# Query weights transposed by DMA, bias rows in two column tiles, FFN weight loads as steps of a new order list

## Chip, cores and metric

The kernel runs on one core of a Trainium2 chip. The metric is the device time of one execution in microseconds (us), the median of several runs. A core has a tensor engine (PE, with its weight loads listed apart as PEld), VectorE (DVE), ScalarE (ACT), GpSimd (POOL) and SyncE (SP); each works through its own queue of instructions in order. In this kernel nearly all DMAs are issued from SP's queue.

## The reference

One transformer block with modulation from a conditioning row. S = 2048 tokens, D = 576, H = 32 heads of 18, FFN width 4608, all in bfloat16:

```python
mod = (silu(c) @ w_mod).reshape(1, 6, 1, D)
sa, ca, ga, sb, cb, gb = (mod[:, i] for i in range(6))
h = layernorm(x) * (1 + ca) + sa
x = x + ga * A(h)
h = layernorm(x) * (1 + cb) + sb
out = x + gb * (relu(h @ w1) @ w2)

def A(h):
    q, k, v = split_heads(h @ wqkv)                    # 32 heads of 18
    pq, pk = q @ w_phi[head], k @ w_phi[head]          # 18 x 18 for each head
    phi_q = concat(softmax(pq), softmax(-pq))          # 36 features
    phi_k = concat(softmax(pk), softmax(-pk))
    kv, z = sum_s(phi_k * v), sum_s(phi_k)             # linear attention, not causal
    return merge_heads((phi_q @ kv) / (phi_q @ z + 1e-6)) @ wo
```

## The kernel before

**Tiles and stages.** The 2048 tokens are 16 tiles t of 128; two tiles make a unit of 256 tokens (n = 0 to 7), four make a block of four tiles. A first phase folds the weights, projects keys and values of all tiles, takes the key softmaxes, sums KV over all tokens and does unit 0 of attention and FFN. Then `block(n)`, n = 1 to 7, does the FFN of unit n with the attention of unit n + 1 between. The seven blocks take the last 272 us of the span, from 151.7 us on. The change lies in the first phase.

**The order of the work.** The first phase is a string of steps, `order`; each word names a function in the table `steps`, with its arguments behind dots, and emits its instructions at once. Each engine runs its instructions in this order, SP's DMAs among them; a semaphore holds an instruction until its operands are there, and all that is queued behind it on that engine waits too. So a word's place in the list fixes where its work stands in every queue.

**Folded weights.** The head maps `w_phi` and the modulation (1 + ca, sa) are folded into the projections, so that one product of the normalized, transposed tile (`hT`) gives the features. For the keys: load the raw rows (`LK.i`), transpose them on PE in six groups of 108 columns, that is six heads (`WT.ci`, `fold_T`, L320; `GRP` has the group starts), copy them to SBUF (`WTE`, L85 on ACT or L87 on DVE, tile `wT`), multiply each group with a block-diagonal matrix of its heads' maps (`F1.ci`, `fold`, L330; the matrix `wbd` is made by `WBD`, `feature_maps`), copy out (`FA1`, `FB1`, into `wplain`), scale by 1 + ca (`SC1`, into `wfold[1]`). For the queries: load the raw rows (`LQ`, 648 KB in two DMAs into a part of the tile `room`), then `QT.ci`, `QTE`, `F0.ci`, `FA0`, `FB0`, `SC0` in the same way, into `wfold[0]`. The value weights are only scaled (`SCv`). There are five row chunks ci, of 128 rows, the last of 64.

**Bias rows.** The shift sa, multiplied with the unscaled folded weights, makes one further row of each folded weight (row 64 of chunk 4, met by a constant 1 in `hT`). `B1`, `Bv`, `B0` (`fold_bias`, L350) compute it for keys, values and queries: two halves of 288 columns by five chunks, ten products with a left operand `sal` of 65 columns, of which only the last holds sa; `BE1`, `BEv`, `BE0` copy that row out on ACT, both halves at once.

**Tiles to transposed tiles.** `LS` statistics, `RS` the root, `LX` the normalized tile `xn`, then `LT.t` a transposing DMA of SP (L227) or, for units 0 and 1, `PT` on PE. `LP` and `LP4` load x for two and four tiles, `LA` and `LM` the modulation weights, `LV` the value weights, `WOL` the output weights. `K.t`, `V.t`, `Q.t` (`project`, `proj`, L406) are ten products each; `KE`, `VE`, `QE` copy them out on ACT.

**From KV to the FFN of unit 0.** `KVa`, `KVb`, `KVc` sum keys by values (L585), `KVE` copies them to SBUF with the heads' mask. `qT.n` transposes the query features of unit n with two DMAs (L613, tile `ET`); `NU.j`, `NV.j` (L626) multiply them with KV for units 0 and 1, and `NUE`, `NVE` divide on DVE (L634 to L641). `WS.ci` scales the output weights (`wo_sb`, L372) by a row that lives in the tile group `wm`; the next tile group at that address holds the FFN weights `w1a` and `w1c`, so their load waits for the last `WS`. `WO`, `WP` are output products. `G.g` (L759, L767) is the first FFN product of group g with its pairs of 64-row products that read `w1c`; `FW.q` (L767) the further ones, q up to 4 on `w1a`, later ones on `w1b`. `Y.j.h.p` (L810) is the second FFN product of tile j, half h, twelve of the 36 chunks k in part p; it reads `w2` (tile `w_sb`), of which each load brings nine chunks.

**FFN weight loads before.** `W1` (`weights_1`, L717 to L719) opens the tiles and issues at once two DMAs for `w1c` and two for `w1a` (8 and 12 of its 20 column blocks); `P2` (`open_p2`, L739, L742) issues the one for `w1b` and four for `w2`. All stand in SP's queue with `qT.1` behind them.

Of the kernel before, what the change touches and what calls it, by code (L numbers as in the profile page):

```python
# [43 lines left out]
def kernel(  # L44
# [271 lines left out]
    def fold_T(which, ci):  # L316

        ps = pool_tiles["T", which, ci] = mm_tile("ps_wT")[:, 0].bitcast(BF16)
        for g, h0 in enumerate(GRP):
            T_.transpose(ps[0:G6, g * P:(g + 1) * P], wraw[which][:, ci, h0 * DH:h0 * DH + G6], ident[:])  # L320
# [24 lines left out]
    def fold_bias(which, src):  # L345

        ps = pool_tiles["B", which] = mm_tile("ps_bias")
        for half in range(2):
            for ci in range(KC):
                T_.matmul(ps[0:65, half, 0:288], lhsT=sal[:, ci, :], rhs=src[:, ci, half * 288:(half + 1) * 288],  # L350
                          start=(ci == 0), stop=(ci == KC - 1))
# [358 lines left out]
    def weights_1():  # L710
# [4 lines left out]
        w1r = B_w1[512:576, :].rearrange("k (j e n) -> k j e n", e=2, n=P)  # L715
        for e in range(2):
            nc.sync.dma_start(w1["c"][e * 64:e * 64 + 64], w1r[:, :, e, :])  # L717
        for lo, hi in ((0, 8), (8, JH)):
            nc.sync.dma_start(w1["a"][:, :, lo * P:hi * P],  # L719
                              B_w1[0:512, lo * P:hi * P].rearrange("(k p) n -> p k n", p=P))  # L720

# [11 lines left out]
    def open_p2():  # L733
# [5 lines left out]
        nc.sync.dma_start(w1["b"][:], B_w1[0:512, JH * P:].rearrange("(k p) n -> p k n", p=P))  # L739
        p2t["w2"] = p2.tile([P, NJ, D], BF16, name="w2_sb")  # L740
        for q in range(4):
            nc.sync.dma_start(p2t["w2"][:, q * 9:(q + 1) * 9, :],  # L742
                              B_w2[q * 9 * P:(q + 1) * 9 * P, :].rearrange("(j p) d -> p j d", p=P))
# [258 lines left out]
```

## Time and profile before

| what | value |
|---|---|
| time, median of 3 runs (lowest to highest) | 425.34 us (425.01 to 426.44) |
| the profiled execution's own time | 425.97 us |
| its span, first to last instruction | 423.6 us |
| granted TensorE clock | 1.00 |

Busy time in stretches of the span, from the trace, in us:

| stretch | PE | DVE | ACT | DMA share |
|---|---|---|---|---|
| 0 to 24 | 19.79 | 17.32 | 15.60 | 0.96 |
| 24 to 48 | 21.58 | 19.90 | 15.13 | 0.73 |
| 48 to 88 | 40.00 | 38.63 | 37.83 | 0.09 |
| 88 to 130 | 40.17 | 26.24 | 24.52 | 1.04 |
| 130 to 160 | 29.89 | 19.72 | 5.33 | 0.30 |
| 160 to 424 | 260.77 | 111.57 | 78.11 | 0.20 |

The first two rows are loading and folding, the third projections and softmaxes, the fourth KV and unit 0 with the FFN weights coming in. The rest are the seven blocks. A row's busy time against its length says how long an engine stood still there; which wait that was is read from the waits of that stretch. A DMA share near 1 says that the sixteen DMA engines always had packets under way. The page lists 4030 products on PE.

### The profile page before, as it was taken

To read this page: it belongs to the slowest core of one execution; us is meant where nothing else is said; L and a number is where in the kernel's file an instruction comes from. 1 tells how busy PE (TensorE), PEld (TensorE's weight loads), DVE (VectorE), ACT (ScalarE), POOL (GpSimd) and SP (SyncE) were. 2 spreads that over 40 slices of the span, in tenths; PEclk is the share of its full clock that TensorE was granted. 3 is DMA by queue.
4 is the path that set the end of the run, shared out by engine and by line. 5 is a ranking of instruction groups with operands and counts; after the bars stand their busy time and mean duration, and the time that the engine had idled before them with its cause. 6 is when DMAs were issued, how large, how long until landed. Compare 5 with 4: busy or idle time off the path is not lost.

```text
span 423.6 us, 9341 instructions
## 1 busy us (share of the span) xinstructions
PE 412.2 (97%) x4030; PEld 338.5 (80%) x4030; DVE 233.4 (55%) x613; ACT 176.5 (42%) x282; POOL 14.6 (3%) x41
## 2 busy tenths in 40 slices
PE   6988999999998999999999999999999999999997
PEld 5876777787786788878878887888888788878886
DVE  6879899999616574528462834555284623230011
ACT  4767899965742126204520540262045204402400
POOL 8300000000000000000000000000000000000000
...
DMA  8997130059995401232041207201420412010000
GB/s 245 355 225 126 33 62 2 2 72 323 380 316 100 102 16 33 33 82 46 2 83 46 33 2 115 31 17 31 84 47 2 84 44 33 2 45 15 2 2 28
DMA packets 68105, 34.90 MB, mean 82 GB/s; under 512 B 53985, under 2 KB 65314, under 8 KB 68066
## 3 DMA queue, kind: packets, MB, share of 16 engines
...
HBM read 19.64 MB, written 2.36 MB: 52 GB/s over the span
## 4 chain that ended last, share of the span: by engine, by line
PE 84%; DMA 7%; SPq 5%; DVE 2%; ACT 1%; issue 0%; DVEq 0%
PE ps_y L810 33%; PE ps_h L767 26%; SPq L742 4%; PE ps_v L406 4%; PE ps_h L759 4%; PE ps_k L406 4%; PE ps_q L406 3%; DMA ET<-room 3%; PE ps_wo L683 3%; PE ps_sum L472 3%; DMA hT<-xn 2%; PE ps_kv L585 1%; DMA oT<-o_tm 1%; PE ps_num L626 1%; PE ps_wo L406 1%; PE ps_bias L350 1%
## 5 line engine op out<-in xcount | busy, mean ns | idle before, releaser
L772 ACT ACTIVATE H<-ps_h 128x1024 bf16<-128x1024 f32 x72 | 73.6, 1022 | 179.0 <-PE ps_h L759 123.8
L810 PE MATMUL ps_y<-w_sb,H 128*128 128x288 bf16 (+2 forms) x1188 | 142.8, 282 | 0.0
L810 PEld LDWEIGHTS <-H 128*128 128x128 bf16 x1188 | 113.7, 98 | 27.3
L767 PE MATMUL ps_h<-hT,w1a 128*128 128x256 bf16 x640 | 74.9, 273 | 0.4 <-DVE hT L377 0.4
L767 PEld LDWEIGHTS <-w1a 128*128 128x128 bf16 x640 | 61.4, 98 | 9.7 <-issue 2.4
L818 DVE TENSOR_TENSOR outt<-ps_y,row_gb 128x288 bf16<-128x288 f32 (+2 forms) x33 | 14.8, 448 | 87.3 <-PE ps_y L810 87.3
L767 PE MATMUL ps_h<-hT,w1b 128*128 128x256 bf16 x512 | 59.2, 273 | 0.0
L406 PEld LDWEIGHTS <-hT 128*128 128x128 bf16 x480 | 46.2, 97 | 13.8 <-DMA hT<-xn 2.1
L767 PEld LDWEIGHTS <-w1b 128*128 128x128 bf16 x512 | 49.7, 98 | 6.8 <-issue 0.8
L688 DVE TENSOR_TENSOR x_sb<-x_sb,ps_wo 128x288 bf16<-128x288 bf16 x28 | 12.7, 454 | 34.3 <-PE ps_wo L683 24.8
L203 DVE BATCH_NORM_STATS2 bst<-x_sb 128x6 f32<-128x288 bf16 x64 | 25.8, 445 | 0.9 <-DMA x_sb<-in_A_x_dram 0.9
L212 DVE TENSOR_SCALAR xn<-x_sb,mv,rstd 128x576 bf16<-128x576 bf16 x32 | 12.3, 430 | 21.0 <-ACT rstd L208 21.0
L406 PE MATMUL ps_v<-wv_sb,hT 128*128 128x288 bf16 x160 | 21.7, 286 | 1.1 <-DMA hT<-xn 1.1
L406 PE MATMUL ps_k<-wfold,hT 128*128 128x270 bf16 (+1 forms) x160 | 21.1, 285 | 0.6 <-DMA hT<-xn 0.6
L406 PE MATMUL ps_q<-wfold,hT 128*128 128x270 bf16 (+1 forms) x160 | 21.3, 285 | 0.0
L759 PE MATMUL ps_h<-hT,w1c 64*128 64x256 bf16 x288 | 19.9, 271 | 0.0
L465 ACT ACTIVATE room<-room 128x1188 bf16<-128x1188 bf16 x16 | 19.0, 1187 | 1.6 <-DVE room L438 1.1
L465 ACT ACTIVATE phik<-phik 128x2376 bf16<-128x2376 bf16 x8 | 17.4, 2181 | 0.3 <-DVE phik L438 0.3
L482 DVE TENSOR_REDUCE ln_s<-room 128x66 f32<-128x1188 bf16 x12 | 16.4, 1363 | 0.0
L759 PEld LDWEIGHTS <-w1c 64*128 64x128 bf16 x288 | 12.1, 94 | 5.2 <-issue 3.8
L425 DVE TENSOR_TENSOR tree<-tree 128x264 bf16<-128x264 bf16 (+2 forms) x48 | 14.6, 304 | 1.7
L634 DVE TENSOR_SCALAR rq<-ps_num 128x24 f32<-128x24 f32 (+1 forms) x18 | 3.0, 177 | 20.1 <-PE ps_num L626 20.1
...
## 6 DMA issues: line engine op xcount, KB each, us to landing
w_sb<-in_B_w_dram SPq DMA_DIRECT2D x4, 1296.0 KB, 18.4
...
w1b<-in_B_w_dram SPq DMA_DIRECT2D x1, 2048.0 KB, 15.3
...
```

The costliest lines, as they stand in the source:

```text
L203: V.bn_stats(out=st[:, half, :], in_=x_sb[:, t0 + j, half * 288:(half + 1) * 288])
L406: T_.matmul(ps[:, 0:cn], lhsT=lhs[:, ci, :], rhs=w[:, ci, cs:cs + cn], start=(ci == 0), stop=(ci == KC - 1))
L425: V.tensor_tensor(out=a[:, :, 0:w], in0=a[:, :, 0:w], in1=a[:, :, w:2 * w], op=op)
L465: A_.activation(out=E[:, j:j + k], in_=E[:, j:j + k], func=ACT.Exp)
L472: T_.matmul(ps, lhsT=ident[:], rhs=e[:, :, :, f * G2:(f + 1) * G2], start=(f == 0), stop=(f == DH // 2 - 1))
L482: V.tensor_reduce(out=t["l", 0][:, j * 22:(j + 1) * 22].rearrange("p (g s) h -> p g s h", s=2), op=ALU.add, axis=mybir.AxisListType.X, in_ ...
L742: nc.sync.dma_start(p2t["w2"][:, q * 9:(q + 1) * 9, :], B_w2[q * 9 * P:(q + 1) * 9 * P, :].rearrange("(j p) d -> p j d", p=P))
L759: T_.matmul(f1[q][:, e, hh * w:hh * w + w], lhsT=w1["c"][r, 2 * q + hh, :], rhs=hT[r, 4, :], start=(first and hh == 0), stop=(not first an ...
L767: T_.matmul(f1[q][:, e, hh * w:hh * w + w], lhsT=w1_at(4 * q + 2 * hh + e, ci), rhs=hT[:, ci, :], start=(first and hh == 0 and ci == 0), s ...
L772: A_.activation(out=p2t["H1"][:, 4 * q:4 * q + 4, :].rearrange("p (h e) n -> p e h n", e=2), in_=f1[q][:].rearrange("p e (h n) -> p e h n" ...
L810: T_.matmul(ps[:, 0, 0:cn], lhsT=p2t["H1"][:, k, j * P:(j + 1) * P], rhs=p2t["w2"][:, k, c], start=(k == 0), stop=(k == NJ - 1))
L818: V.tensor_tensor(out=o[:, c], in0=ps[:, 0, 0:cn], in1=rows["gb"][:, c], op=ALU.mult)
```

## The change

1. **Query weights.** `LQ` is now six steps. Each is one transposing DMA that reads 128 columns of `A_wqkv` in DRAM, from column 108 g on, and writes group g of `wqT`. The load of the raw query rows, `QT` and `QTE` are gone; `fold_T` serves the keys alone. So that the groups start at equal distances, the last one starts at head 30 instead of 26: the key rows are padded with zeros to 668 columns, and the last group of `wph` holds only two heads' maps, with zeros behind.
2. **Bias rows.** The left operand `sal` is one column. The two halves of each bias row go to PSUM partition 64 and to partition 0, and their products alternate. Each half is copied out by its own step, on DVE (`.0` at the end) or ACT (`.1`).
3. **FFN weights.** `W1` and `P2` open the tiles only. `LW.0` and `LW.1` load the halves of `w1c`, `LW.2` and `LW.3` those of `w1a`, `LW.4` loads `w1b`, `W2.q` a quarter of `w2`.
4. **The order list** is another one throughout. Among much else, x and the key rows are loaded in another order, all `WS` come around and behind `KVc`, `LW.3` is the first of the FFN weights, `W2.1` stands behind `qT.1`, and one step `Z.8` adds one product on zeros. `block` is as before.

```diff
-GRP = [0, 6, 12, 18, 24, 26]
+GRP = [0, 6, 12, 18, 24, 30]
 KK = [P, P, P, P, 64]
 NGR = len(GRP)
 G6 = 6 * DH
+DX = 5 * G6 + P
...
-    wv_raw, wq_raw, wqT = part(0, KC, D), part(KC * D, KC, D), part(2 * KC * D, NGR, D)
-    wq_plain = part((2 * KC + NGR) * D, KC, D)
-    o = (3 * KC + NGR) * D
-    wbd, sal = part(o, NGR, G6), part(o + NGR * G6, KC, 65)
+    wv_raw, wqT, wq_plain = part(0, KC, D), part(6752, NGR, D), part(10208, KC, D)
+    o = KC * D
+    wbd, sal = part(o, NGR, G6), room[:, o + NGR * G6:o + NGR * G6 + KC]
...
-    wraw = {1: p0.tile([P, KC, D], BF16, name="wk_raw"), 0: wq_raw}
+    wk_raw = p0.tile([P, KC, DX], BF16, name="wk_raw")
...
+    V.memset(wph[:, 5, :], 0.0)
...
-    A_.dma_start(wph[0:G6, 5, :], wphr[D - G6:])
+    A_.dma_start(wph[0:36, 5, :], wphr[5 * G6:])
...
-            nc.sync.dma_start(wraw[1][:, 2 * i:2 * i + 2, :], rows)
+            nc.sync.dma_start(wk_raw[:, 2 * i:2 * i + 2, 0:D], rows)
         else:
-            nc.sync.dma_start(wraw[1][0:64, 4, :], A_wqkv[512:576, D:2 * D])
+            nc.sync.dma_start(wk_raw[0:64, 4, 0:D], A_wqkv[512:576, D:2 * D])
+
+    def load_turned(which, g):
+        c0 = which * D + g * G6
+        nc.sync.dma_start_transpose(out=wT[which][:, g, :], in_=A_wqkv[:, c0:c0 + P])
...
-    zero_rows(wraw[1])
+    G.memset(wk_raw[:, :, D:], 0.0)
+    G.memset(wk_raw[64:128, 4, 0:D], 0.0)
...
-        for g, c, h, nh in ((slice(0, 5), 0, 0, 3), (slice(0, 5), GF, 3, 3), (slice(5, 6), 0, 4, 2)):
+        for g, c, h, nh in ((slice(0, 5), 0, 0, 3), (slice(0, 5), GF, 3, 3), (slice(5, 6), 0, 0, 2)):
...
-        V.tensor_copy(out=sal[:, 0:4, 64], in_=mod_ps[1][:, 0:4])
-        V.tensor_copy(out=sal[0:64, 4, 64:65], in_=mod_ps[1][0:64, 4:5])
+        V.tensor_copy(out=sal[:, 0:4], in_=mod_ps[1][:, 0:4])
+        V.tensor_copy(out=sal[0:64, 4:5], in_=mod_ps[1][0:64, 4:5])
...
-    def fold_T(which, ci):
-
-        ps = pool_tiles["T", which, ci] = mm_tile("ps_wT")[:, 0].bitcast(BF16)
-        for g, h0 in enumerate(GRP):
-            T_.transpose(ps[0:G6, g * P:(g + 1) * P], wraw[which][:, ci, h0 * DH:h0 * DH + G6], ident[:])
-
-    def fold_T_out(which, ci, eng):
-        copy(eng, wT[which][0:G6, :, ci * P:ci * P + KK[ci]],
-             pool_tiles["T", which, ci][0:G6, 0:NGR * P].rearrange("p (g c) -> p g c", c=P)[:, :, 0:KK[ci]])
+    def fold_T(ci):
+
+        ps = pool_tiles["T", ci] = mm_tile("ps_wT")[:, 0].bitcast(BF16)
+        for g in range(NGR):
+            T_.transpose(ps[0:G6, g * P:(g + 1) * P], wk_raw[:, ci, g * G6:(g + 1) * G6], ident[:])
+
+    def fold_T_out(ci, eng):
+        copy(eng, wT[1][0:G6, :, ci * P:ci * P + KK[ci]],
+             pool_tiles["T", ci][0:G6, 0:NGR * P].rearrange("p (g c) -> p g c", c=P)[:, :, 0:KK[ci]])
...
-        for half in range(2):
-            for ci in range(KC):
-                T_.matmul(ps[0:65, half, 0:288], lhsT=sal[:, ci, :], rhs=src[:, ci, half * 288:(half + 1) * 288],
+        for ci in range(KC):
+            for half in range(2):
+                p = 64 - half * 64
+                T_.matmul(ps[p:p + 1, half, 0:288], lhsT=sal[:, ci:ci + 1], rhs=src[:, ci, half * 288:(half + 1) * 288],
                           start=(ci == 0), stop=(ci == KC - 1))
 
-    def fold_bias_out(which, dst):
-        copy(A_, dst[64:65, 4, :].rearrange("p (a n) -> p a n", a=2), pool_tiles["B", which][64:65, :, 0:288])
+    def fold_bias_out(which, dst, half, eng):
+        p = 64 - half * 64
+        copy(eng, dst[64:65, 4, half * 288:(half + 1) * 288], pool_tiles["B", which][p:p + 1, half, 0:288])
...
-        w1r = B_w1[512:576, :].rearrange("k (j e n) -> k j e n", e=2, n=P)
-        for e in range(2):
-            nc.sync.dma_start(w1["c"][e * 64:e * 64 + 64], w1r[:, :, e, :])
-        for lo, hi in ((0, 8), (8, JH)):
+
+    def load_w1(i):
+        if i < 2:
+            w1r = B_w1[512:576, :].rearrange("k (j e n) -> k j e n", e=2, n=P)
+            nc.sync.dma_start(w1["c"][i * 64:i * 64 + 64], w1r[:, :, i, :])
+        elif i < 4:
+            lo, hi = ((0, 8), (8, JH))[i - 2]
             nc.sync.dma_start(w1["a"][:, :, lo * P:hi * P],
                               B_w1[0:512, lo * P:hi * P].rearrange("(k p) n -> p k n", p=P))
+        else:
+            nc.sync.dma_start(w1["b"][:], B_w1[0:512, JH * P:].rearrange("(k p) n -> p k n", p=P))
+
+    def load_w2(q):
+        nc.sync.dma_start(p2t["w2"][:, q * 9:(q + 1) * 9, :],
+                          B_w2[q * 9 * P:(q + 1) * 9 * P, :].rearrange("(j p) d -> p j d", p=P))
...
-        nc.sync.dma_start(w1["b"][:], B_w1[0:512, JH * P:].rearrange("(k p) n -> p k n", p=P))
...
-        for q in range(4):
-            nc.sync.dma_start(p2t["w2"][:, q * 9:(q + 1) * 9, :],
-                              B_w2[q * 9 * P:(q + 1) * 9 * P, :].rearrange("(j p) d -> p j d", p=P))
...
-        "WT": lambda p: fold_T(1, p), "WTE": lambda g, a=0: fold_T_out(1, g, VA[a]),
-        "QT": lambda p: fold_T(0, p), "QTE": lambda g, a=0: fold_T_out(0, g, VA[a]),
+        "WT": fold_T, "WTE": lambda g, a=0: fold_T_out(g, VA[a]),
...
+        "LV": lambda: load_rows(nc.sync, wv_raw, A_wqkv, 2 * D, 3 * D), "LQ": lambda ci: load_turned(0, ci),
...
-        "BE1": lambda: fold_bias_out(1, wfold[1]), "BEv": lambda: fold_bias_out("v", wv_sb),
-        "BE0": lambda: fold_bias_out(0, wfold[0]), "OPEN": open_p1,
+        "BE1": lambda h, a=0: fold_bias_out(1, wfold[1], h, VA[a]), "BEv": lambda h, a=0: fold_bias_out("v", wv_sb, h, VA[a]),
+        "BE0": lambda h, a=0: fold_bias_out(0, wfold[0], h, VA[a]), "OPEN": open_p1,
...
-    LK.0 WT.0 WT.1 WBD LK.1 SIL WTE.1.1 WTE.0.0 WT.3 LP.0 WTE.3.1 LS.0 LS.1 LK.2 F1.0 FB1.0.1 LA.1 WT.2 WTE.2.0
-    LA.0 WT.4 WTE.4.0 FA1.0.1 RS.0 F1.3 FA1.3.1 FB1.3.1 LV F1.1 F1.2 LX.0 FA1.2.1 FB1.2 FB1.1 MC1.1 MSC SC1.3
-    PT.0 PTB.0 SC1.0 MC1.0 MSH FA1.1.1 F1.4 SCv.1 SCv.3 PTA.0 Bv LP.1 LQ SCv.0.1 FA1.4.1 LP4.2 SCv.2.1 FB1.4.1
-    SCv.4 CR BEv SC1.4.1 SC1.1 B1 BE1 V.1 QT.1 LS.3 LS.2 SC1.2 OPEN LS.6 LS.7 VE.1 QTE.1.1 K.1 RS.1 KE.1 V.0
-    QT.3 LX.1 RS.3 VE.0 QTE.3.1 K.0 KE.0 QT.0 LM.1 MC2.2 MC2.3 LX.3 LS.5 F0.1 FA0.1.1 MC2.1 QTE.0.0 PT.1 LS.4
-    FB0.1.1 PTA.1 PTB.1 QT.2 QTE.2.0 QT.4 QTE.4.0 MC2.0 LM.2 LP4.6 MC2.4 F0.2 RS.2 LS.15 FB0.2.1 LT.6 K.6 K.2
-    KE.6 FA0.2 LP4.4 F0.0 KE.2 V.3 FA0.0.1 SC0.2 WOL LS.9 LT.7 F0.3 LX.2 FB0.0 LT.5 LS.8 VE.3 FA0.3 RB LT.4 RS.4
-    LM.0 FB0.3.1 RBE K.3 LS.11 LX.4 SC0.1.1 V.7 KE.3 F0.4 LS.10 VE.7 SC0.0.1 FA0.4.1 K.4 RS.5 MN.0 FB0.4.1 B0
...
-    LO.7 HI.7 V.6 EX.6 qSA.0 EX.7 SC.0 Q.14 Q.7 VE.6 qRC.0 SU.6 SC.2 SA.4 SU.7 SC.5 V.11 RC.4 SA.6 WS.3 qSC.0
-    QE.7 WS.4 SA.7 QE.14 SC.4 RC.6 Q.4 SC.6 QE.4 RC.7 SC.7 qT.0 VE.11 WS.2 qMN.1 KVa KVb KVc Q.13 KVE.0.1 QE.13
-    KVE.1 NU.1 NUE.1 Q.5 QE.5 NU.0 OT.1 Q.11 NUE.0 QE.11 qLO.1 Q.6 OTE.1 qMX.1 qHI.1 OT.0 W1 WO.1 WOE.1 S2.1
-    QE.6 OTE.0 qEX.3 WO.0 WOE.0 S2.0 Q.12 Q.15 QE.12 qMN.2 Q.10 Q.9 P2 R2 qEX.2 X2 QE.15 PN PNE QE.10 qLO.2 QE.9
-    G.0 RL.0 qMX.2 qHI.2 qEX.5 qSU.1 qSA.1 qRC.1 FW.2 RL.2 FW.1 RL.1 G.1 FW.5 RL.3 qSC.1 qT.1 RL.5 FW.4 RL.4 G.2
-    RL.6 FW.7 RL.7 qSD.5 NV.0 Y.0.0.0 NVE.0 Y.0.0.1 NV.1 OU.0 qEX.4 Y.0.1.0 Y.0.1.1 qSD.4 NVE.1 qRC.2 OU.1 qSC.2
-    qT.2 WP.0 WPE.0 FW.8 RL.8 WP.1 WPE.1 Y.0.0.2 S3.0 Y.0.1.2 S3.1 R3 X3 XT Y.1.0.0 YE.0.0 YE.0.1 MD.3 MD.2
-    Y.1.0.1 MD.4 Y.1.0.2 YE.1.0 MD.0 MD.1 Y.1.1.0 Y.1.1.1 Y.1.1.2 YE.1.1
...
+    LK.2 LP.0 LK.0 WT.0 LS.1 LS.0 WTE.0.0 WT.4 WTE.4.0 RS.0 LX.0 SIL LK.1 WT.1 WBD WT.3 PT.0 PTB.0 LP.1 WTE.1.1
+    WTE.3.1 LS.2 LA.0 F1.1 FB1.1 PTA.0 WT.2 WTE.2.0 LA.1 FA1.1.1 Z.8 LQ.0 F1.0 LV FB1.0.1 F1.4 FA1.0.1 LS.3
+    FA1.4.1 CR LQ.1 MC1.0 F1.3 MSH FB1.4.1 F1.2 FB1.2 MC1.1 MSC SC1.0 LQ.4 FA1.3.1 FA1.2.1 SC1.2 SC1.1 FB1.3.1
+    SC1.3 B1 BE1.1.0 SC1.4.1 BE1.0.1 LP4.2 Bv SCv.0.1 RS.1 K.1 BEv.1.0 LQ.2 SCv.2.1 K.0 LQ.3 SCv.3 LP4.4 LQ.5
+    BEv.0.1 OPEN KE.1 KE.0 SCv.4 LX.1 PT.1 SCv.1 V.0 V.1 PTA.1 VE.0 VE.1 LS.6 PTB.1 F0.2 FB0.2.1 V.3 LS.7 RS.3
+    LS.5 FA0.2 VE.3 LS.11 F0.1 FA0.1.1 FB0.1.1 K.3 F0.3 LX.3 LS.4 FA0.3 KE.3 LS.8 FB0.3.1 SC0.1.1 RS.2 K.2 KE.2
+    F0.4 LM.2 RB LS.10 LX.2 F0.0 LM.1 MC2.4 MC2.3 FB0.0 FA0.4.1 MC2.0 LT.7 LS.9 LM.0 RS.5 FB0.4.1 SC0.2 V.7
+    SC0.3 SC0.4 RBE LT.6 MX.0 FA0.0.1 K.7 SC0.0.1 LT.4 B0 BE0.1.0 VE.7 RS.4 KE.7 BE0.0.1 MN.0 LO.1 K.6 KE.6 LT.5
+    K.5 Q.2 LX.5 HI.1 KE.5 QE.2 LP4.6 LS.13 LS.12 LX.4 Q.1 LS.15 QE.1 LT.10 LT.11 EX.1 LT.8 LS.14 MC2.2 V.4 VE.4
...
+    Q.4 V.14 SA.6 SU.7 SC.4 SA.7 KVa RC.6 SC.6 WS.0 RC.7 SC.7 KVb WS.1 VE.14 KVc KVE.1 QE.4 Q.11 KVE.0.1 NU.1
+    WS.2 WS.4 QE.11 NUE.1 Q.5 NU.0 NUE.0 QE.5 OT.1 OTE.1 WS.3 Q.12 W1 LW.3 OT.0 OTE.0 qMX.1 qHI.1 LW.2 WO.1 LW.1
+    WOE.1 S2.1 WO.0 WOE.0 QE.12 S2.0 Q.9 QE.9 Q.6 QE.6 R2 Q.15 Q.10 P2 X2 QE.15 W2.2 PN PNE QE.10 LW.0 G.0 RL.0
+    qMN.1 qLO.1 qEX.3 qMN.2 FW.2 qEX.2 FW.1 qSU.1 RL.1 qMX.2 RL.2 W2.0 qHI.2 qSA.1 qRC.1 LW.4 G.1 RL.3 qLO.2
+    qEX.5 FW.4 FW.5 qSC.1 RL.4 RL.5 W2.3 G.2 FW.7 qT.1 qEX.4 qSD.4 RL.6 NV.0 W2.1 FW.8 RL.8 NVE.0 NV.1 NVE.1
+    OU.0 Y.1.0.0 Y.1.0.1 WP.0 qSD.5 RL.7 Y.1.0.2 OU.1 WPE.0 WP.1 WPE.1 S3.1 Y.0.0.0 Y.1.1.0 Y.1.1.1 qRC.2
+    Y.0.0.1 qSC.2 YE.1.0 S3.0 R3 Y.0.0.2 X3 XT MD.2 MD.0 MD.3 MD.1 Y.0.1.0 MD.4 qT.2 Y.1.1.2 Y.0.1.1 Y.0.1.2
...
```

More of the change, by code (lines that the diff above doesn't have):

```diff
@@ L180 @@
         G.memset(xn[:, :, D:D + 1], 1.0)
-    zero_rows(wma, wplain[1], wv_raw, wfold[1], wv_sb, wraw[0], wmb, wplain[0], wfold[0])
+    zero_rows(wma, wplain[1], wv_raw, wfold[1], wv_sb, wmb, wplain[0], wfold[0])
     G.memset(wo_sb[:, 4, :], 0.0)
@@ L861 @@
         "RB": lambda: mod_row("gb", 3), "RAE": lambda: mod_row_out("ga"), "RBE": lambda: mod_row_out("gb"), "WS": wo_scale,
-        "W1": weights_1, "LM": load_mods, "WOL": load_wo, "KVa": kvs(0, 12), "KVb": kvs(12, 14), "KVc": kvs(14, NT), "KVE": lambda i, a=0: kv_out(i, VA[a]),
+        "W1": weights_1, "LW": load_w1, "W2": load_w2, "LM": load_mods, "WOL": load_wo, "KVa": kvs(0, 12), "KVb": kvs(12, 14), "KVc": kvs(14, NT), "KVE": lambda i, a=0: kv_out(i, VA[a]),
         "NU": lambda j: num(0, j), "NUE": lambda j: quotient(0, j), "OT": lambda j: o_T(0, j),
@@ new lines @@
+    K.5 Q.2 LX.5 HI.1 KE.5 QE.2 LP4.6 LS.13 LS.12 LX.4 Q.1 LS.15 QE.1 LT.10 LT.11 EX.1 LT.8 LS.14 MC2.2 V.4 VE.4
+    LT.9 K.4 KE.4 Q.3 Q.0 QE.3 LO.0 RS.7 HI.0 QE.0 MN.1 V.2 VE.2 qMN.0 RS.6 WOL LX.7 LT.15 V.8 VE.8 V.10 VE.10
+    K.10 KE.10 LX.6 K.11 KE.11 MC2.1 RA V.9 EX.0 RAE K.9 LO.2 MX.1 HI.2 VE.9 LO.3 HI.3 KE.9 K.8 KE.8 MN.2 LO.4
+    K.15 MCE2 LT.14 qLO.0 Q.8 EX.3 QE.8 LT.12 Q.14 KE.15 QE.14 qMX.0 qHI.0 SU.3 V.15 SU.0 SA.0 EX.2 VE.15 K.14
+    RC.0 LT.13 SA.3 RC.3 MX.2 HI.4 K.12 SU.2 SC.0 KE.14 LO.5 qEX.0 KE.12 qEX.1 K.13 V.13 KE.13 HI.5 V.5 VE.13
@@ new lines @@
+    SA.2 MX.3 EX.5 RC.2 VE.5 MN.3 EX.4 LO.7 V.11 V.12 SU.1 SA.1 LO.6 VE.12 qSU.0 qSA.0 Q.7 RC.1 VE.11 HI.6 SC.2
+    QE.7 SC.3 SU.5 EX.6 SU.4 qRC.0 HI.7 Q.13 QE.13 SA.5 RC.5 V.6 SC.1 SU.6 SA.4 SC.5 EX.7 VE.6 qSC.0 qT.0 RC.4
+    Q.4 V.14 SA.6 SU.7 SC.4 SA.7 KVa RC.6 SC.6 WS.0 RC.7 SC.7 KVb WS.1 VE.14 KVc KVE.1 QE.4 Q.11 KVE.0.1 NU.1
+    WS.2 WS.4 QE.11 NUE.1 Q.5 NU.0 NUE.0 QE.5 OT.1 OTE.1 WS.3 Q.12 W1 LW.3 OT.0 OTE.0 qMX.1 qHI.1 LW.2 WO.1 LW.1
+    WOE.1 S2.1 WO.0 WOE.0 QE.12 S2.0 Q.9 QE.9 Q.6 QE.6 R2 Q.15 Q.10 P2 X2 QE.15 W2.2 PN PNE QE.10 LW.0 G.0 RL.0
```

8 lines of the change are left out of this document (1 added, 7 removed).

## Prediction

> **What bounds the kernel now.** First the page's busy shares and its row of DMA shares:
>
> ```profile
> PE 412.2 (97%) x4030; PEld 338.5 (80%) x4030; DVE 233.4 (55%) x613; ACT 176.5 (42%) x282; POOL 14.6 (3%) x41
> ...
> DMA  8997130059995401232041207201420412010000
> ```
>
> PE is busy for 412.2 of 423.6 us, so a change pays only by taking work or waits off PE's queue. The DMA engines are full in two stretches, the first 24 us and from 88 to 130 us; the change works in both. Next, PE's waits (line, releaser: us in total, times, longest):
>
> ```profile
> PE ps_num L626 <- DMA ET<-room: 1.5, 1, 1.5
> PE ps_wT L320 <- DMA wk_raw<-in_A_wqkv_dram: 1.4, 1, 1.4
> PE ps_fold L330 <- DVE wT L87: 1.2, 1, 1.2
> ...
> PE ps_v L406 <- DMA hT<-xn: 1.1, 1, 1.1
> PE ps_fold L330 <- DVE room L87: 0.7, 1, 0.7
> PE ps_k L406 <- DMA hT<-xn: 0.6, 1, 0.6
> ```
>
> All lie before 130 us. The three that end on transposed tiles (1.5, 1.1, 0.6) came behind loads in SP's queue. Between 24 and 48 us PE stands idle for 2.4 us in all (windows 24:28 1.26, 28:32 0.08, 36:40 0.92, 40:48 0.17); from 48 to 88 us PE is never idle, with DVE and ACT at 94 to 96%. Third, PE's timeline (start, length, then the group):
>
> ```profile
> 13.76 2.61 PE L350 MATMUL ps_bias<-room 128*65 128x288 bf16 x10
> 16.16 1.51 PE L350 MATMUL ps_bias<-wk_plain,room 128*65 128x288 bf16 x10
> 17.51 1.39 PE L406 MATMUL ps_v<-wv_sb,hT 128*128 128x288 bf16 x10
> 18.73 0.50 PE L320 MATMUL ps_wT<-ident,room 128*108 128x128 bf16 x6
> 19.07 1.39 PE L406 MATMUL ps_k<-wfold,hT 128*128 128x270 bf16 x10
> ```
>
> From start to start, ten bias products of 288 columns took 2.40 us at 13.76, and ten value products of 288 columns 1.22 us at 17.51: until about 16.6 us PE runs at half pace, though the clock row says 1.00. One query step of six transposes takes 0.34 us.
>
> Fourth, what a transposing DMA does to loads behind it (stretch, busy of PE, PEld, DVE, ACT, POOL, clock, DMA share, GB/s):
>
> ```profile
> 24.50:25.00 0.50, 0.50 (x15) 0.50 (x12) 0.47 (x3) 0.50 (x2) 0.00 (x0) 1.00 0.12 34
> ...
> 26.50:27.00 0.50, 0.00 (x0) 0.00 (x0) 0.50 (x3) 0.00 (x0) 0.00 (x0) 1.00 0.04 3
> ...
> 28.00:28.50 0.50, 0.42 (x4) 0.37 (x5) 0.49 (x2) 0.00 (x0) 0.00 (x0) 1.00 1.09 442
> ```
>
> One transpose was issued at 22.26, loads from 23.61 on. The transpose lands at 28.07, after 5.8 us where the pair at 42.48 takes 2.6 each, and the loads flow only from 28.0. Behind the two transposes of 31.3 the flow of the load issued at 33.87 starts at about 36. So a turn from transposing to loading leaves the engines empty for some 1 to 1.8 us, and a transpose itself holds them 0.8 to 1.0 us (164 KB at 160 to 200 GB/s, 42 to 46 us).
>
> Fifth, SP's queue for the FFN weights, and what flowed:
>
> ```profile
> 93.68 1.34 SPq L717 DMA_DIRECT2D w1c<-in_B_w_dram  x2
> 95.07 1.80 SPq L719 DMA_DIRECT2D w1a<-in_B_w_dram  x2
> 96.98 0.64 SPq L739 DMA_DIRECT2D w1b<-in_B_w_dram  x1
> 97.72 19.25 SPq L742 DMA_DIRECT2D w_sb<-in_B_w_dram  x4
> 117.14 8.03 SPq L613 DMA_TRANSPOSE ET<-room  x1
> ```
> ```profile
> 94.00:97.00 3.00, 3.00 (x42) 2.36 (x39) 2.48 (x10) 1.67 (x5) 0.00 (x0) 1.00 0.97 193
> ...
> 99.00:106.00 7.00, 7.00 (x61) 5.53 (x60) 6.43 (x16) 4.73 (x10) 0.00 (x0) 1.00 1.03 391
> ```
>
> The w1b load lands 15.3 us after its issue, at 112.3; the first three of w2 after 18.4, 20.9 and 14.3, at 116.1, 119.9 and 123.6: in order of issue, one each 3.8 us. A small load behind a big one waits for the big one.
>
> **The change, part by part.**
>
> *Query transposes by DMA.* Off PE: five steps of 0.34 us, 1.7 us. Off ACT and DVE: five evictions (0.80, 0.80, 0.56, 0.56, 0.35), hidden by PE either way. Onto SP: six transposes for the plain load of 648 KB. Each costs SP about 1.3 us of issue (hT<-xn: 1.30 at 22.26). No row transposes from DRAM. Below: 147 KB as a plain load at 390 GB/s, 0.4 us, no gap. Above: the hT row, 1.0 us, with 1.8 us of gap at each of the four places where LV, LP4.2, LP4.4 and LM.2 follow. I take 1.0 us and a gap of 1 us, the nearest row, for the opcode is the same.
>
> SP issues LQ.0 behind LA.1. By the flow of before (2.6 MB by 10.3 us) its data starts at 10.3; then LQ.0, gap, LV 1.9, LQ.1 and LQ.4 2.0, gap, LP4.2 1.6, LQ.2 and LQ.3 2.0, gap, LP4.4 1.6, LQ.5 1.0: 24.4, landed at about 25.5 (21 by the lower bound, 28.4 by the upper). F0.2, the first query fold, needs all six. Before it PE has K.1, K.0, PT.1, V.0, V.1 from 17.5 on: 4 x 1.23 + 0.6 = 5.5, so it is due at 23.0. The wait is about 2.5 us, and everything queued on PE behind it waits too. Behind LQ.5 stand LM.2, LM.1 (landed 32), LT.7, LM.0, LT.6, LT.5, for V.7, K.6 and K.5: about 1 us more. New waits: 3.5 us (0 to 8).
>
> *Early order.* The key rows come third, not first: by the flow (0.66 MB by 4.4 us, plus 0.85 us to land) WT.0 starts at 5.25 instead of 4.03. DVE does two tiles' statistics (2.0), two evictions (0.9), LX.0 (0.96) and SIL (0.8) ahead of WBD, so the first fold is due at 9.5 instead of 7.39, but 24 key transposes and PT.0 are then behind it. The rest (five folds, WT.2, two MC1, one fill of 0.43) brings B1 to 15.0. B1 and Bv were 20 products in 3.85 us; as pairs side by side at half pace they are 10 x 0.24 = 2.4, to 17.4. Against 17.51: nothing won or lost. Bounds: 0.6 us won if PE is at full pace by then; 2.4 lost if the pairs do not run side by side.
>
> *B0 as pairs*: 10 x 0.123 = 1.23 becomes 0.62; 0.6 won (0 if one after the other). Six evictions of half a row replace three of 0.64 on ACT: under PE.
>
> *The idle 2.4 us* of 24 to 48 us belonged to the old queue and goes with it. Early sum: -1.7 - 0.6 - 2.4 + 3.5 = -1.2 us (-4.7 to +3.3).
>
> *FFN weights as steps.* C is the end of KVc (94.2 before). W1's first load waits for the last WS, which reads the tile that w1a replaces. Before, WS.2 ends before C, and SP issues at C - 0.5. Now WS.3 stands behind NUE.0 on DVE: KVE.1 and two WS to C + 1.4, NUE.1 from C + 2.0 and NUE.0 to C + 5.1 (1.5 each, as at 95.83 and 97.38), WS.3 to C + 5.6. The queue starts 6 us later against C, in the order w1a (1.57 MB), w1a (1.05), half w1c, W2.2, half w1c, W2.0, w1b, W2.3, two ET, W2.1. PE reaches G.0 at C + 14.2 (before C + 15.1, with one query product of 1.23 more behind C), and its pairs, which read both halves of w1c, at C + 16. With w1a at 391 GB/s 6.6 us, w1c at 193 1.5 each, W2.2 3.8, start 0.5 and 0.9 to land, the second half lands at C + 20.4: a wait of 4.4 us. From there to the tenth product of Y, which needs W2.1, PE has 19.2 us of work: C + 39.7. W2.1 lands later: 6.1 + 6.6 + 3.0 + 4 x 3.8 + 5.3 (w1b) + 3.6 (two ET, 360 KB at 200 GB/s) + 1 (gap) + 0.9 = C + 41.7. Before, PE stood there at C + 38.1 (NV.0 at 128.78, FW.8 1.75, NV.0 and NV.1 0.7, nine products 1.1). Shift: the query product charged back, 1.2 + 41.7 - 38.1 = +4.8 by the transfers, 1.2 + 39.7 - 38.1 = +2.8 by PE alone. I take +3.9 (+1.3, with w1c at 391 GB/s and ET hidden, to +6).
>
> *After 160 us* block is the same; nothing hides or adds there.
>
> Sum: -1.2 + 3.9 = +2.7 us on the span of 423.6, so 426.3; its execution took 425.97, 0.6 above the median of 425.34. The forecast is 425.3 + 2.7 = **428.0 us**, with 426.7 to 430.5 as its own range.
>
> **Two rules against these rows.** The half pace until 16.6 us is a row; the Trainium skill (TensorE: Matmul & The Clock Gate, Part 1) has the array's clock halved until one free-running window of about 3.4 us has been busy. By that rule one-row products after a less dense stretch could move the change of pace one window on, and K.1 and K.0 would lose 1.2 us; with F0.2 waiting for its transposes that falls into the wait. The second rule is at rival A.
>
> **Rivals.**
> A, faster: the transposes cost no more than loads. For it: their six strips are only 147 KB each. Against: the empty stretches above. Then no new early waits, -4.7, and the late stage by PE alone, +2.8: 423.4. The Trainium skill (Advanced Engine Details and Errata, X-Bar Transpose (TRN2)) says that transposing DMAs are as fast as regular ones, 350 to 400 GB/s; the rows at 160 to 200 GB/s do not agree, though none reads DRAM.
> B: the late weights are hidden, because loads share the engines rather than follow each other. Against: landings 3.8 us apart in order of issue. Then -1.2 + 0: 424.1.
> C, slower by much: a transpose from DRAM in 256-byte rows takes twice the hT row, 2 us. F0.2 then waits until 32, the tiles behind it likewise: 6 us more than the forecast's half-hidden case less 1 that the mods' later loads hide, +5: 433.
> D: the pairs do not run side by side, so that part does nothing: +0.6 for B0 and up to 2.4 for B1 and Bv, half of it inside the wait at F0.2: 430.
>
> **Chances.** Forecast 0.45, A 0.22, B 0.10, C 0.18, D 0.05. A measurement here tells about 0.3% (1.3 us) from nothing. Two thirds of A and half of B are faster, the rest of these within 0.3%: faster 0.20, same 0.13, slower 0.67. The range, 423.4 to 433.0, cuts off half of A below and half of C above.
>
> **What would show it.** In the new profile: PE waiting at F0.2 (ps_fold) on room<-in_A_wqkv_dram for 2 to 3 us near 23 to 26 us; ps_h at the pairs waiting for w1c 3 to 5 us; ps_y waiting on w_sb once, about 2 us; no L320 on room; bias pairs starting together. If the w1c wait is missing, the late part is wrong; if F0.2 does not wait, A holds.

## The result, and the profile after

The changed kernel takes 432.6 us, median of four runs (432.4 to 433.47); the kernel before took 425.83 beside it. The ratio is 1.0157 (95% interval 1.0137 to 1.0176): 6.8 us slower. Its profiled execution has a span of 430.0 us, 6.4 more than before.

The page of the changed kernel, busy shares and rows of the granted clock and the DMA share:

```profile
PE 411.0 (96%) x4000; PEld 335.2 (78%) x4001; DVE 236.5 (55%) x614; ACT 174.7 (41%) x280; POOL 15.0 (3%) x41
...
PEclk9999999999789999999999999999999999999999
DMA  8976420037997071062015205011411321010000
```

PE does 1.2 us less and the span is longer, so the time went into waits. The clock row has a dip in the eleventh and twelfth slice (107 to 129 us) that the row of before does not have. Its waits on PE:

```profile
PE ps_h L772 <- DMA w1c<-in_B_w_dram: 6.0, 1, 6.0
PE ps_wT L326 <- DMA wk_raw<-in_A_wqkv_dram: 3.3, 1, 3.3
PE ps_h L780 <- ACT room L86: 1.9, 1, 1.9
...
PE ps_y L823 <- DMA w_sb<-in_B_w_dram: 0.6, 1, 0.6
```

The third line names ACT, whose copy was early; the same wait is named `w1a` in e1 and e3. No line names a DMA into `room`, so none waits for the query weights. PE's timeline (start, length, group) and stretches of 1 us (PE, PEld, DVE, ACT, POOL busy, clock, DMA share, GB/s) at the long wait:

```profile
108.71 1.92 PE L780 MATMUL ps_h<-hT,w1a 128*128 128x256 bf16 x16 [1.88 <-ACT room L86]
116.65 1.46 PE L772 MATMUL ps_h<-hT,w1c 64*128 64x256 bf16 x12 [6.02 <-DMA w1c<-in_B_w_dram]
118.04 4.82 PE L780 MATMUL ps_h<-hT,w1a 128*128 128x256 bf16 x32
```
```profile
112.00:113.00 1.00, 0.00 (x0) 0.00 (x0) 0.93 (x3) 0.00 (x0) 0.00 (x0) 1.00 1.09 345
113.00:114.00 1.00, 0.00 (x0) 0.00 (x0) 0.86 (x5) 0.00 (x0) 0.00 (x0) 0.80 1.30 205
114.00:115.00 1.00, 0.00 (x0) 0.00 (x0) 0.64 (x1) 0.00 (x0) 0.00 (x0) 0.50 1.29 162
...
119.00:120.00 1.00, 1.00 (x7) 0.69 (x6) 0.00 (x0) 1.00 (x2) 0.00 (x0) 0.50 1.07 403
120.00:121.00 1.00, 1.00 (x9) 0.82 (x8) 0.00 (x0) 0.48 (x1) 0.00 (x0) 0.78 1.06 414
```

Three us into the wait, at 113.6 (the row from 113 reads 0.80, so 0.6 us at full clock and 0.4 at half), the granted clock falls to half, and it stays there until about 120.4, 3.8 us after work is back. From start to start, the 12 pair products and the 32 products behind them take 1.39 and 4.66 us; at full clock the same work takes 0.76 and 3.5 (e1): 1.8 us more. SP's queue for the FFN weights:

```profile
98.45 0.93 SPq L730 DMA_DIRECT2D w1a<-in_B_w_dram  x2
99.44 0.59 SPq L727 DMA_DIRECT2D w1c<-in_B_w_dram  x1
100.14 4.43 SPq L736 DMA_DIRECT2D w_sb<-in_B_w_dram  x1
104.61 3.81 SPq L727 DMA_DIRECT2D w1c<-in_B_w_dram  x1
```

The first load goes out at 98.45, before at 93.68, although KV ends earlier (the query product behind it starts at 92.81, before at 94.17). The second half of `w1c` stands behind 1.3 MB of `w2`.

The first 25 us on PE:

```profile
16.18 1.36 PE L357 MATMUL ps_bias<-wk_plain,room 128*1 128x288 bf16 x10
17.33 1.13 PE L357 MATMUL ps_bias<-room 128*1 128x288 bf16 x10
18.39 2.62 PE L414 MATMUL ps_k<-wfold,hT 128*128 128x270 bf16 x20
21.67 1.01 PE L241 MATMUL psT_h<-ident,xn 128*128 128x128 bf16 x10 [0.65 <-DVE xn L218]
22.52 2.61 PE L414 MATMUL ps_v<-wv_sb,hT 128*128 128x288 bf16 x20
24.97 0.43 PE L336 MATMUL ps_fold<-room 108*128 108x108 bf16 x6
...
35.31 0.78 PE L357 MATMUL ps_bias<-room 128*1 128x288 bf16 x10
36.02 2.62 PE L414 MATMUL ps_k<-wfold,hT 128*128 128x270 bf16 x20
```

The bias pairs run side by side: the ten products of B0, at full pace, take 0.71 us (35.31 to 36.02) where ten took 1.22 before. The first ten take 1.15, at half pace, as e10 confirms. The first query fold, at 24.97, waits for nothing.

**Where the 6.4 us went.** From the end of KV to the first block it is 64.8 us (92.81 to 157.61), before 57.4 (94.17 to 151.54): 7.4 more. Up to the end of KV it is 1.4 us less, and in the blocks 0.3 more. The late part by PE's own rows: waits of 0.3, 1.9, 6.0 and 0.6 and the half clock 1.8, 10.6 in all, for 1.9 of before, less one query product (1.2) that is now done ahead of KV.

### The profile page after: what moved, and what is told of

Read it like the earlier page. It is cut to its first block, busy times and chain, and to the rows that moved or that the text cites. A ratio compares the mean times of both kernels' runs of the same rounds, so it can differ in the third digit from the quotient of the medians.

```text
span 430.0 us, 9293 instructions
## 1 busy us (share of the span) xinstructions
PE 411.0 (96%) x4000; PEld 335.2 (78%) x4001; DVE 236.5 (55%) x614; ACT 174.7 (41%) x280; POOL 15.0 (3%) x41
## 4 chain that ended last, share of the span: by engine, by line
PE 86%; DMA 5%; DVE 4%; ACT 2%; SPq 1%; issue 1%; ACTq 0%
PE ps_y L823 33%; PE ps_h L780 27%; PE ps_v L414 4%; PE ps_h L772 4%; PE ps_q L414 4%; PE ps_k L414 3%; DMA w1c<-in_B_w_dram 3%; PE ps_wo L691 3%; PE ps_sum L480 3%; DMA w_sb<-in_B_w_dram 2%; PE ps_wo L414 2%; PE ps_kv L593 1%; DVE bst L209 1%; SPq L621 1%; PE ps_num L634 1%; DMA x_sb<-in_A_x_dram 1%
## 5 line engine op out<-in xcount | busy, mean ns | idle before, releaser
L780 PE MATMUL ps_h<-hT,w1a 128*128 128x256 bf16 x640 | 76.2, 275 | 1.9 <-ACT room L86 1.9
L86 ACT ACTIVATE phik<-ps_k 128x540 bf16<-128x540 f32 (+1 forms) x32 | 11.5, 416 | 3.3 <-PE ps_k L414 3.2
```

The costliest lines, as they stand in the source:

```text
L780: T_.matmul(f1[q][:, e, hh * w:hh * w + w], lhsT=w1_at(4 * q + 2 * hh + e, ci), rhs=hT[:, ci, :], start=(first and hh == 0 and ci == 0), s ...
```

## The experiments

Theory at the start: the late loss is the load queue, by its order or by its late start; the early part gains a little. Ratios are to the kernel before, run beside each on the same chip.

**e1**, the second half of `w1c` ahead of `w2`:

```diff
-WO.1 LW.1 WOE.1 ... QE.10 LW.0 G.0
+WO.1 LW.1 LW.0 WOE.1 ... QE.10 G.0
```

> The changed kernel with one load moved: the second half of w1c is issued right behind the first, ahead of the first w2 load. Times stand against 432.6 us of the changed kernel (span 430.0). Theory T (the loss is the order inside the load queue, and a half of w1c that flows alone takes 2.8 us where two together take 3.0): w1a has flowed by 107.3, both halves by 110.3, landed by 111, where the pairs are due at 110.6; the wait of 6.0 us on w1c and the half clock behind it (1.8 us) go, but w1b, still behind two w2 loads, lands near 124 and is due near 120.6: a new wait of some 3.3 us, 427 to 428 us. Rival R1 (nothing else is late): 424.8. Rival R2 (the queue starts too late and every byte ahead of the last w2 load counts, so the wait only moves): 430 or more, with ps_y waiting on w_sb for 3 us or more.

431.45 us, ratio 1.0115 (1.0055 to 1.0175). PE's waits:

```profile
PE ps_h L780 <- DMA w1b<-in_B_w_dram: 3.2, 1, 3.2
...
PE ps_y L823 <- DMA w_sb<-in_B_w_dram: 2.5, 1, 2.5
PE ps_h L772 <- DMA w1c<-in_B_w_dram: 2.1, 1, 2.1
PE ps_h L780 <- DMA w1a<-in_B_w_dram: 1.8, 1, 1.8
```

These are 9.6 us where the changed kernel waited 8.5: the wait moved, as R2 said, though `w_sb` took 2.5 us and not 3. The halves, adjacent, flowed from 107.3 to about 111.7, 4.4 us; apart, in the changed kernel, they took about 2.8 each (by the low rates from 107.0 and from 113.2), so being together saves 1 us and not 2.6.

**e2**, the order of need from the same start:

```diff
-... LW.3 ... LW.2 ... LW.1 ... W2.2 ... LW.0 ... W2.0 ... LW.4 ... W2.3 ... qT.1 ... W2.1
+... LW.1 LW.0 ... LW.2 ... LW.3 ... LW.4 W2.0 ... qT.1 W2.1 W2.2 W2.3
```

> The changed kernel with the FFN loads in the order in which PE needs them, from the same start of the queue: both halves of w1c, the smaller w1a, the larger w1a, w1b, w2 quarter 0, the two transposes for ET, then w2 quarters 1, 2, 3. Theory T (the order inside the queue is the whole late loss; its start, 5.6 us behind the end of KV, is not): the waits on w1a (1.9), w1c (6.0), w_sb (0.6) and the half clock (1.8) all go but for 0.7 us on w1a at the second product group: span 420 to 421, time 422.5 to 424, under the kernel before. Rival R2 (the late start binds): a wait of 2 us or more is left on w1b, ET or w_sb, and the time stays above 426.

433.28 us, 1.0147 (1.0081 to 1.0212): no better. The waits on `w1c` and on the first `w1a` went; 1.2 us came on `w1a`, 3.1 on `w_sb`, 3.2 on the transposed tile of the output product, and the clock halved at 134. Order alone does not help.

**e3**, work without a use inside the wait:

```diff
         f1_whole(0, qs[0], True)
+        if g == 0:
+            ps = aux_tile("ps_warm")
+            for _ in range(24):
+                T_.matmul(ps[:], lhsT=ident[:], rhs=wo_sb[:, 0, 0:512], start=True, stop=True)
```

> The changed kernel with 24 products of 128x128 by 128x512 without a use put on PE between the first FFN product group and its pairs, where PE waits for w1c: some 5.2 us of work inside the wait of 6.0 us. It computes the same. Theory T (the half clock from 113.7 to 120.4 us comes from the idle 6 us and costs 1.8 us of its own): the granted clock stays 1.00, w1c lands when it did, and the time falls by 1.5 to 2 us, to 430.6 to 431.1. Rival R3 (the clock falls for another reason, or what follows waits anyway for w1b and w2): within 0.5 us of 432.6.

431.78 us, 1.0107 (1.0048 to 1.0165), span 429.9: the time does not decide. In this execution the clock fell earlier, at 109.4, just behind the wait of 2.3 us for `w1a` (same columns as above):

```profile
108.00:109.00 1.00, 0.00 (x0) 0.00 (x0) 0.97 (x4) 0.84 (x3) 0.00 (x0) 1.00 1.33 146
109.00:110.00 1.00, 0.71 (x4) 0.57 (x5) 0.90 (x4) 0.00 (x0) 0.00 (x0) 0.70 1.11 238
110.00:111.00 1.00, 1.00 (x7) 0.70 (x5) 0.97 (x3) 0.00 (x0) 0.00 (x0) 0.50 1.08 348
```

The first product group took 3.3 us instead of 1.9, so the 24 products ended 1.3 us late. Behind them the clock is 1.00, and from the first pair to the first product on `w1b` it is 9.9 us (117.99 to 127.87) where the changed kernel needs 11.7 (116.65 to 128.31). So the half clock's 1.8 us is real; what filling saves was not shown.

**e4**, bias rows in one column tile (the products of the kernel before; the copies by halves stay):

```diff
-                T_.matmul(ps[p:p + 1, half, 0:288], lhsT=sal[:, ci:ci + 1], ...)
+                T_.matmul(ps[0:65, half, 0:288], lhsT=sal[:, ci, :], ...)
```

> The changed kernel with the bias rows as before: a left operand of 65 columns, halves one after the other in one column tile; each half is still copied out by its own step. Theory T (the two halves run side by side): B1 and Bv take about 4.5 us where they took 2.2, B0 1.2 where it took 0.7; of these 2.8 us the wait of 0.65 for the second normalized unit hides a part: 1.5 to 2.5 us more by the end of KV; of that the late wait on w1c, whose loads start behind KV, hides nothing: 434 to 435.2. Rival D (the halves run one after the other in both): within 0.4 us of 432.6.

433.42 us, 1.0151 (1.0095 to 1.0208). The end of KV comes 1.2 us later (94.03), less than expected, and the profiled span is 1.3 longer (431.3). e10 asks again without late waits.

**e5**, the queue started earlier, its order kept:

```diff
-... KVb WS.1 VE.14 KVc KVE.1 ... WS.2 WS.4 ... OTE.1 WS.3 Q.12 W1 LW.3 ... LW.2 WO.1 LW.1
+... KVb WS.1 WS.2 WS.4 WS.3 VE.14 KVc W1 LW.3 LW.2 LW.1 KVE.1 ...
```

> The changed kernel with the queue of FFN loads started earlier and its order unchanged: the last three steps that scale the output weights run on DVE ahead of the copy of KV, and the two w1a loads and the first half of w1c follow at once. The queue should start near 93.5 us instead of 98.45. Theory S (the late start of the queue is the late loss, since its bytes flow one after the other): everything in it lands 4.9 us earlier; the wait on w1a (1.9) and the half clock (1.8) go, the wait on w1c falls from 6.0 to about 3.0: span 423 to 424.5, time 425.5 to 427. Rival O (the order inside the queue is the loss and the wait moves on): a new wait of 2 us or more on w1b or w_sb, time above 429.5. If the DVE work put ahead of the copy of KV costs PE, NU.1 waits for KVZ by more than 0.3 us.

430.03 us, 1.0105 (1.0063 to 1.0148). The queue starts at 93.69, 4.8 us earlier; the wait on `w1a` is gone, that on `w1c` is 4.5 us and halves the clock once more. Better, but by less than half of the 5.6 to 7.1 us that were expected: with both halves of `w1c` apart, the second still landed at 114.2. As feared, the DVE work ahead of the copy of KV costs PE a little: `NU.1` waits 0.7 us for it, before 0.3.

**e6**, both, and `WP.0` behind `Y.1.0.2`:

> As e5_early_start, and the loads in the order of need as well: both halves of w1c, the smaller w1a, the larger, w1b, w2 quarters 0 and 1, the two transposes for ET, quarters 2 and 3; one output product stands behind the third part of its neighbour's second FFN product. Theory S: with the start near 93.5 no late wait above 0.7 us is left but for about 1 us on the transposed tile of the output product: span 419.5 to 421.5, time 422 to 424, below the kernel before by 2 to 4 us. Rival O: as e2_need_order, the waits come back on w_sb or on transposes behind w2 loads, time above 427.

425.03 us, 0.9983 (0.9959 to 1.0006), span 421.6: level with the kernel before, where 422 to 424 was expected. Order alone moved the median by +0.7 us, start alone by -2.6, both by -7.6 (by the ratios, which allow for the chip, -0.4, -2.2 and -7.4). Neither theory alone holds: an early start is of little use unless what comes first is what PE needs first, and the right order of none while the queue is late as a whole. The 7.6 is not of order and start alone, though: e6 also moves `WP.0`, for whose tile e2 waited 3.2 us, and issues `W2.1` ahead of the transposes for `ET`. What these two moves give by themselves was not run. One late wait of size is left, 1.7 us on `w_sb`. The empty stretch ahead of it, and then the second of its rows as it is in e8:

```profile
117.00:118.00 1.00, 1.00 (x11) 0.90 (x10) 0.30 (x1) 1.00 (x2) 0.00 (x0) 1.00 0.20 67
118.00:119.00 1.00, 1.00 (x12) 0.90 (x10) 0.00 (x0) 0.82 (x2) 0.00 (x0) 1.00 0.36 79
```
```profile
118.00:119.00 1.00, 1.00 (x12) 0.90 (x11) 0.40 (x1) 1.00 (x2) 0.00 (x0) 1.00 1.08 355
```

In e6 SP stood at the transposes for `ET`, which wait for DVE, and almost nothing was under way (67 and 79 GB/s, in e8 355).

**e7** and **e11**, the query weights on PE. `LQ` loads 648 KB plainly, five steps transpose it on PE, five evictions follow; e7 on the changed kernel, e11 on e8 with the steps spread differently:

```diff
+            T_.transpose(ps[0:G6, g * P:(g + 1) * P], room[:, o:o + G6], ident[:])
...
-LQ.0 ... LQ.1 ... LQ.4 ... LQ.2 ... LQ.3 ... LQ.5
+LQ ... QT.2 QTE.2 ... QT.1 QTE.1 ... QT.3 QTE.3 ... QT.0 QTE.0 ... QT.4 QTE.4
```

> The changed kernel with the query weights loaded plainly (648 KB, in place of the first of the six transposing DMAs; the other five are gone) and transposed on PE in five steps of six, with five evictions on ACT and DVE. Theory T (the transposing DMAs from DRAM are hidden: F0.2 waited for nothing): PE has 1.7 us more, and the evictions (0.35 to 0.8 each, 3.1 us in all) press on ACT and DVE, which were 90% busy there: the end of KV comes 1.7 to 3 us later, span 431.7 to 433, time 434.2 to 435.5. Rival A (DMAs that turn from loading to transposing hold up the tiles behind them, and this costs what PE wins): within 0.7 us of 432.6 or faster.

> As e8_w2_before_et, with the query weights loaded plainly and transposed on PE as in e7_query_on_pe, the five steps now spread from the value bias row on, three of the evictions on DVE and none in a place where PE waits for it at once. Theory T: PE's 1.7 us and half of the evictions' 3.1 us reach the end: 425 to 427. Rival A: the six transposing DMAs cost as much elsewhere as they take off PE: within 0.7 us of 423.1. If it is 428 or more, as in e7_query_on_pe, the evictions and not PE's transposes are what the DMAs save.

e7 takes 437.78 us, 1.0275 (1.0223 to 1.0327), its KV ends 6.0 us later than in the changed kernel (0.6 of it was there at its first key transpose); e11 429.49, 1.0063 (1.0040 to 1.0085), where e8 has 0.9926; its KV ends 5.4 us later than in e8, and a wait of 1.0 us for `ET` is new. Both lose more than PE's 1.7 us: between 24 and 40 us PE stands still for 2.9 us in either, where e8 has 0.4, because products wait for copies out of PSUM that ACT or DVE has not yet made, of their operand or of a tile that they are to overwrite:

```profile
29.71 1.15 PE L429 MATMUL ps_v<-wv_sb,hT 128*128 128x288 bf16 x8 [0.63 <-DVE hT L88]
...
31.78 1.39 PE L429 MATMUL ps_k<-wfold,hT 128*128 128x270 bf16 x10 [0.66 <-ACT v L86]
```

(PE's timeline of e11.) It is the places in the queues and not a lack of time: in e11 DVE itself stood still for 3.2 us up to 28.04, at the copy of a query transpose that PE reached at 27.50, with the copy of `hT` queued behind it. The size holds for these two places of the steps; the kernel before does the same work on PE with smaller waits. e7 also prices the DMAs. The early loads, the same but for the queries, flow until 27.0 us in the changed kernel and until about 24.2 in e7:

```profile
26.00:27.00 1.00, 1.00 (x15) 0.86 (x13) 0.97 (x3) 0.72 (x3) 0.00 (x0) 1.00 1.01 338
27.00:28.00 1.00, 1.00 (x11) 0.78 (x9) 0.97 (x5) 0.92 (x3) 0.00 (x0) 1.00 0.08 18
```
```profile
23.00:24.00 1.00, 1.00 (x18) 0.91 (x17) 0.14 (x1) 1.00 (x3) 0.28 (x1) 1.00 0.98 332
24.00:25.00 1.00, 1.00 (x11) 0.80 (x9) 0.00 (x0) 1.00 (x3) 0.00 (x0) 1.00 0.52 117
```

So the six transposes with their turns cost 2.8 us more than the plain load, which by the rates of these stretches is 1.7 to 2.1 us: 4.5 to 4.9 in all, from one execution of each, which differ by 0.6 us already at the first key transpose.

**e8**, **e9**, **e10** on e6. e8 issues `W2.2` ahead of `qT.1`; e9 is e8 with `WBD` ahead of `SIL`; e10 is e8 with the bias rows of e4:

```diff
-W2.0 W2.1 ... qSC.1 qT.1 W2.2 W2.3
+W2.0 W2.1 W2.2 ... qSC.1 qT.1 W2.3
```

> As e6_both, with w2 quarter 2 issued ahead of the two transposes for ET instead of behind them. In e6_both the DMA engines stood empty from 117 to 119 us, because SP waited for the scaled queries with nothing behind it under way, and the last w2 quarter came 1.7 us late. Theory S: quarter 2 fills that gap, ET lands near 124.5, when it is due at 124.7, quarter 3 near 129.5, due at 130.6: the wait of 1.7 us goes and the time falls to 423 to 424. Rival: ET comes late instead (NV.0 waits 1 us or more), within 0.7 us of 425.0.

> As e8_w2_before_et, with the block-diagonal head maps made ahead of the gate of the conditioning row on DVE (0.9 us earlier). In the changed kernel the first fold waited 0.6 us (1.1 in e6_both) for these maps; the gate is needed only by the modulation products 3 us later. Theory: the first fold comes 0.6 us earlier, and as the stretch behind it is bound by ACT and DVE as well, 0.3 to 0.6 us of that reach the end: 422.5 to 423.7. Rival (evictions and transposes bind there): within 0.2 us of e8_w2_before_et.

> As e8_w2_before_et (423.1 us), where no late load is waited for, with the bias rows as before: 65 columns, one column tile, halves one after the other. In e4_bias_65 this put the end of KV 1.2 us later, but the time rose by only 0.8. Theory T: with nothing late to hide it, the 1.2 us reach the end: 424.0 to 424.8. Rival: the stretch from 24 to 88 us, bound by DVE and ACT, takes them up: within 0.4 us of 423.1.

e8: 423.07 us, 0.9926 (0.9900 to 0.9953): the gap and the wait on `w_sb` are gone, as expected, and it beats both kernels. e9: 422.72, 0.9919 (0.9890 to 0.9948): not told from e8, and 0.35 us below it, inside the theory's range and outside the rival's 0.2. The first fold starts 0.8 us earlier (10.19), but 0.7 and 0.9 us of new waits on ACT and DVE follow, and in these two executions 0.1 us is left at the end of KV (93.02 for 93.14): the traces speak for the rival, the times do not decide. e10: 424.88, 0.9949 (0.9924 to 0.9973), span 422.9 to e8's 420.8. Its bias rows on PE, with e8's:

```profile
16.11 2.59 PE L356 MATMUL ps_bias<-wk_plain,room 128*65 128x288 bf16 x10
18.50 2.60 PE L356 MATMUL ps_bias<-room 128*65 128x288 bf16 x10
20.89 2.81 PE L413 MATMUL ps_k<-wfold,hT 128*128 128x270 bf16 x20
```
```profile
16.18 1.36 PE L357 MATMUL ps_bias<-wk_plain,room 128*1 128x288 bf16 x10
17.33 1.41 PE L357 MATMUL ps_bias<-room 128*1 128x288 bf16 x10
18.67 3.55 PE L414 MATMUL ps_k<-wfold,hT 128*128 128x270 bf16 x20
```

4.8 us for two rows where the pairs take 2.5; with B0, 1.22 for 0.71. Of these 2.8 us, 1.75 are left at the start of KV (89.82 for 88.07) and about 1 to 2 at the end. The pairs are worth that.

**e12**, the kernel before with the last `w2` quarter behind `qT.1`:

```diff
-        for q in range(4):
+        for q in range(3):
...
-qSC.1 qT.1 RL.5
+qSC.1 qT.1 LW2 RL.5
```

> The kernel before with one load moved: the last w2 quarter is issued behind the two transposes for ET instead of ahead of them. Theory: the wait of 1.5 us of NV.0 for ET goes, the last quarter lands near 128 and is due near 139: 424.0 to 424.5 where the kernel before takes 425.4. Then e8_w2_before_et beats it by a further 1 us, which is the early stage's. Rival: within 0.4 us of the kernel before, as ET is held up by the two quarters under way.

424.05 us, 0.9932 (0.9905 to 0.9960): the wait of 1.5 us for `ET` is gone. The medians of e12 and e8 are 1.0 us apart, as expected, but on two chips; by their ratios to the kernel before it is 0.3 us, well inside both intervals. So e12 is as good as e8, and e8's lead over the kernel before is no proof that the new early stage is better at the end; one moved load does as much for the old one.

## Why the prediction was right in its sign and wrong in its size

The direction, the place and the first cause were right: the wait on `w1c` stood where it was put, behind a late queue with a half of `w1c` behind `w2`. The size was 2.7 us, measured 6.8.

- *"I take +3.9 (+1.3 ... to +6)" for the late weights* is the term that failed. In the same accounting (the query product charged back) it measured 7.4 + 1.2 = 8.6, outside its own bounds. Three things were missing. The two halves of `w1c` were priced at 1.5 us each from a row where they flow together; apart they took about 2.8 each, and the queue's first us after the issue carried little (49 GB/s from 99 to 100 us, where the sum had 0.5 us of start): the second half landed 23.8 us after KV, not 20.4, while PE was due at 17.8, so the wait was 6.0 and not 4.4. `w1a`, counted as landing in time, was 1.9 late. And an idle PE was priced at its length only, while the half clock that followed, which the sum put at nothing, cost 1.8 more. That the tenth product of Y would wait about 2 us for `W2.1` was too much: 0.6, as PE itself came late.
- *"New waits: 3.5 us" early* did not come: F0.2, due at 23.0 and reached at 24.97, waited for no transpose. The DMAs cost 4.5 to 4.9 us with their turns, where 1.0 us each and four turns of 1 us made 10. Empty stretches beside the transposes do show: the DMA engines moved 89 GB/s from 11.0 to 12.0 us and 7 from 18.0 to 19.0. But of four turns only these two look so, and in the second SP was still issuing the last transpose (from 16.61, for 2.05 us); whether the turn or the issue empties the engines stays open. Rival A, by which nothing waits for them, held for this step.
- *"Nothing won or lost" up to the bias rows* was 0.9 lost (K.1 at 18.39, against 17.51), with 3.3 us of wait for the key rows, before 1.4. (The 20 old products took 3.75 us by the rows shown, not 3.85.) B0 gave 0.5 for 0.6. The old idle time of 2.4 fell to 0.4. With the waits of 0.8 from 20 to 24 us: -1.7 - 0.5 - 2.0 + 0.9 + 0.8 = -2.5, in the forecast's accounting -1.4 - 1.2 = -2.6 by the end of KV. The forecast was -1.2.
- *Rival B* was shut out by the 6.0 us on `w1c`, and by e1 and e2: what is moved ahead makes something else late. *Rival C* named 433 us, near the time, by luck: its wait at F0.2 did not exist. *Rival D* was wrong: the pairs run side by side.
- Two of the wrong prices had one root: a row for one situation (a tile's transpose between loads, two halves flowing together) was used for another. The Trainium skill (Advanced Engine Details and Errata, X-Bar Transpose (TRN2)) puts transposing DMAs at 350 to 400 GB/s; the 885 KB here in 4.5 to 4.9 us are 180 to 200 with the turns counted, so the measurement differs.
